# Attention and the first two experts' weights moved into the list schedule, first blocks in smaller steps, token group 0 always visited first

## The chip, the cores and the metric

One core of a Trainium2 chip runs the whole program: TensorE (PE) for matmuls, VectorE (DVE), ScalarE (ACT) and GpSimd (POOL) for elementwise work, SyncE (SP) for issuing most transfers. The metric is the time on the device in microseconds (us), as the median of three runs. Beside it stands one execution taken with the hardware profiler, whose trace the rows below come from.

## The reference

Three layers follow one another on 2 x 576 = 1152 tokens of width 512: attention over a window of 64 keys, four experts that are all used and weighted by gate probabilities, and a layer that multiplies by a cosine of itself.

```python
scores = scale * np.matmul(q, k.transpose(0, 1, 3, 2))
mask = (rel >= 0) & (rel < window)                # window = 64
attn = softmax(np.where(mask, scores, -1e9))
x = np.matmul(attn, v)                            # 2 x 8 heads x 576 x 64, then 1152 x 512
for e in range(4):                                # w1: 512 x 1024, w2: 1024 x 512
    out += p[:, e:e + 1] * (np.maximum(x @ w1[e], 0.0) @ w2[e])
h = out @ w_in                                    # 512 x 2048
y = (h * np.cos(h)) @ w_out                       # 2048 x 512
```

## The kernel before

**Precision.** Each factor of a large matmul is held as a high and a low part, and a product is three matmuls: high by high, high by low, low by high. A weight (name `raw`) is loaded in float32, its high part (`whi`) is a rounding copy, its low part (`wlo`) the difference.

**Attention.** The 1152 tokens are 18 blocks of 64 queries. For a pair of blocks the scores `pss` (L261) are 16 small matmuls from `kT` and `qt`, where `qt` is the query tile `qraw` in another order (function `att_r`). Per block then follow the scaled and masked scores `s` and their maximum `nm` on VectorE (`att_m`), the exponential `e` with its sums on ScalarE (`att_e`), a reciprocal `ri`, the scaling of `e` on GpSimd (`att_n`), four transposes into `pst` (L310), their copy `pt` out of PSUM, and per pair the values `psv` (L325, 16 small matmuls), which become the high and low half of x (`xhi`, `xlo`).

**Experts.** Each of the four experts and the cosine layer are cut into units of 512 hidden columns: units 0 and 1 are the first expert, 2 to 7 the other three, 8 to 11 the cosine layer. Units 0 and 1 run in the plain way: `emit_a` gives twelve matmuls into `ph` (L432 to L434, L629), `emit_b` three per tile of 128 tokens into `pb_acc` (L470), over three token groups of 256, 384 and 512. From unit 2 on the first product is built from seven products of half size (`y` and `seed`, L1038) with sums of weights (`w7hi`, `w7lo`) and of tokens (`tsum`, `thi`, `tlo`), over two token groups, 0 of 640 and 1 of 512 tokens (products with 320 and 256 columns); the second product is `pb_acc` again (L1232). Between unit 7 and unit 8 the sum over the experts is transposed (`psx`, L1304) to become the new x.

**What sets the order.** Each engine runs its instructions in the order in which they are written and waits at the first one that is not ready. The program has two parts. Up to a step in the last token group of the first expert the order is a hand-written list, the string `ORDER`: each token is a load, a step of attention, a weight half, or a point where the next piece of an expert's matmuls goes (`piece`). `W10` in it is ten filler matmuls (`keep_busy`, L241, `idle_ps`, 128 ones by 128 ones). After that point a list scheduler takes over: each group of instructions is a `Job` with an engine, an assumed duration, what it depends on and the buffers that it takes; `plan` lays the jobs out by their latest start times, with TensorE's jobs in the order of `pe_list` and up to eight ahead, `rehearse` replays a plan with small random delays, and the best of 120 plans is emitted. In that second part `visits` sets which token group of a unit comes first, and it alternates:

```python
    for c in range(SPL, NX):
        ks = (0, 1) if (c % 2 == 0) == (c < NM) else (1, 0)
        visits += [(c, k) for k in ks]
```

**Loads.** The SP queue issues most transfers, in the order of the list; ScalarE's queue issues the first chunk of k and two of the q tiles.

Of the kernel before, what the change touches and what calls it, by code (L numbers as in the profile page):

```python
# [27 lines left out]
def tile_window_attention_moe_cosglu(  # L28
# [14 lines left out]
    B, H, D, S = k.shape  # L43
    NTOK = B * S
# [84 lines left out]
    def split_hi(n, copy=nc.scalar.copy):  # L129
        hi = w_tile(n, "hi")  # L130
        copy(out=hi, in_=raw_t[n])
        w_hi[units[n]] = hi

    half_lo = {}


    def split_lo(n, engine, part=None):
        t, hi = raw_t[n], w_hi[units[n]].bitcast(F32)
        if n not in half_lo:
            half_lo[n] = w_tile(n, "lo")  # L140
        lo = half_lo[n]
        c = t.shape[1] // 2
        cs = slice(None) if part is None else slice(c * part, c * (part + 1))
        engine.tensor_tensor(out=lo[:, cs], in0=t[:, cs], in1=hi[:, cs], op=ALU.subtract)
        if part != 0:
            raw_t.pop(n)
            w_lo[units[n]] = half_lo.pop(n)

    actx = ExitStack()
    kp = actx.enter_context(tc.tile_pool(name="kp", bufs=2))  # L150
    vp = actx.enter_context(tc.tile_pool(name="vp", bufs=4))
# [10 lines left out]
    NQ, NVB = 4, 4  # L162
# [3 lines left out]
    def load_q(j):  # L166
        b, i = divmod(j, BPB)
        t = qp.tile([P, W, NP], F32, tag="qraw", name="qraw")
        queue = nc.scalar if 1 < j < 4 else nc.sync
        queue.dma_start(out=t, in_=q[b, i].rearrange("h d n p -> (h d) n p"))  # L170
        q_t[j] = t

    def att_r(j, copy=nc.gpsimd.tensor_copy):
        t = q_t.pop(j)
        qt = qp.tile([P, NP, W], F32, tag="qt", name="qt")
        copy(out=qt.rearrange("d p n -> d n p"), in_=t)
        qt_t[j] = qt


    KCH = [(0, 3), (4, 6), (7, 8), (9, 11), (12, 14), (15, 17)]  # L180
    KMAX = 5 * W


    def load_k(c):
        a, z = KCH[c]
        b, s = divmod(a * W, S)
        s1 = s + (z + 1 - a) * W
        o = 2 * W - nkeys(a)
        t = kp.tile([P, NP, KMAX], F32, tag="kT", name="kT")
        if o:  # L190
            nc.vector.memset(t[:, :, :o], 0.0)
        (nc.sync if c else nc.scalar).dma_start(
            out=t[:, :, o:(z + 2 - a) * W],
            in_=k[b].rearrange("(p h) d s -> (h d) p s", h=2)[:, :, s - W + o:s1],
        )
        for j in range(a, z + 1):
            k_t[j] = t[:, :, (j - a) * W:(j - a + 2) * W]

    def load_v(j):
        n = nkeys(j)  # L200
        b, s = divmod(j * W, S)
        t = vp.tile([P, H * D], F32, tag="vr", name="vr")
        if n < P:
            nc.vector.memset(t[:P - n], 0.0)
        nc.sync.dma_start(out=t[P - n:], in_=v[b, s + W - n:s + W, :])
        v_t[j] = t
# [60 lines left out]
    def att_m(u):  # L267
        pv = ss_t.pop(u)
        b = u - u % 2
        mask = masks[tuple(c for c in range(2) if (b + c) % BPB == 0)]  # L270
        s = sp.tile([P, NP, 2 * W], F32, tag="s", name="s", bufs=3)
        nc.vector.scalar_tensor_tensor(
            out=s, in0=pv, scalar=SCALE, in1=mask.to_broadcast([P, NP, 2 * W]),
            op0=ALU.mult, op1=ALU.min,
        )
        nm = smp.tile([P, NP], F32, tag="nm", name="nm")
        nc.vector.tensor_reduce(out=nm, in_=s, op=ALU.max, axis=AX.X, negate=True)
        s_t[u] = (s, nm)

    def att_e(u):  # L280
        s, nm = s_t.pop(u)
        e = sp.tile([P, NP, 2 * W], F32, tag="e", name="e", bufs=4)
        sm = smp.tile([P, NP], F32, tag="sm", name="sm")
        for p in range(NP):
            nc.scalar.activation(
                out=e[:, p], in_=s[:, p], func=AF.Exp, bias=nm[:, p:p + 1], scale=1.0,
                accum_out=sm[:, p:p + 1],
            )
        r = smp.tile([P, NP], F32, tag="r", name="r")
        nc.scalar.activation(out=r, in_=sm, func=AF.Identity, bias=bias_e, scale=1.0)  # L290
        e_t[u], sm_t[u] = e, r
# [3 lines left out]
    def att_i(u):  # L295
        r = sm_t.pop(u)
        ri = smp.tile([P, NP, 1], F32, tag="ri", name="ri")
# [3 lines left out]
    def att_n(u):  # L301
        e, ri = e_t.pop(u), ri_t.pop(u)
        nc.gpsimd.tensor_tensor(out=e, in0=e, in1=ri.to_broadcast([P, NP, 2 * W]), op=ALU.mult)
        pn_t[u] = e

    def att_t(u):
        pn = pn_t.pop(u)
        ps = bank("pst").rearrange("m (p t) -> m p t", p=NP)
        for p in range(NP):
            nc.tensor.transpose(out=ps[:, p], in_=pn[:, p], identity=ident)  # L310
        ps_t[u] = ps

    def att_p(u, copy=nc.vector.tensor_copy):
        pt = sp.tile([P, NP, P], F32, tag="pt", name="pt", bufs=3)
        copy(out=pt, in_=ps_t.pop(u))
        pt_t[u] = pt

    def att_v(u):
        pts, vts = ([t.pop(u - 1 + c) for c in range(2)] for t in (pt_t, v_t))
        ps = bank("psv") if u * W >= GS[0] else psb.tile([P, 512], F32, tag="psb", name="psv")  # L320
        pv = ps.rearrange("m (p t) -> m p t", p=NP)
        for c in range(2):
            for p in range(NP):
                for h in range(2):
                    nc.tensor.matmul(  # L325
                        out=pv[W * h:W * (h + 1), p, W * c:W * (c + 1)],
                        lhsT=vts[c][:, P * p + W * h:P * p + W * (h + 1)],
                        rhs=pts[h][:, p, W * c:W * (c + 1)],
                        start=True, stop=True,
                    )  # L330
        o_t[u] = pv

    def att_xhi(u):
        pv, at = o_t[u], (u - 1) * W
        k = max(i for i in range(2) if S0[i] <= at)
        if at == S0[k]:
            x_tiles(k)
        hi, lo = (tokens(x[k], k, (at - S0[k]) // P) for x in (xhi, xlo))
        o_t[u] = pv, hi, lo
        nc.scalar.copy(out=hi, in_=pv)  # L340

    def att_xlo(u):
        pv, hi, lo = o_t.pop(u)
        nc.vector.tensor_tensor(out=lo, in0=pv, in1=hi.bitcast(F32), op=ALU.subtract)


# [52 lines left out]
    queues = {"h": [], "j": [], "f": []}  # L399
    script = []  # L400

    def side(kind, fn, *args):
        if script:
            queues[kind].append((fn, args))
        else:
            fn(*args)


    def piece():
        while script:  # L410
            x = script.pop(0)
            if x == ".":
                break
            token(x)
        if not script:
            for kind in queues:
                while queues[kind]:
                    fn, args = queues[kind].pop(0)
                    fn(*args)

    def emit_a(s):
        e, g, f = steps[s]
# [1359 lines left out]
```

## Time and profile before

| | us |
|---|---|
| median of three runs (629.33 to 630.48) | 630.41 |
| profiled execution | 630.69 |
| its span, first to last instruction | 628.9 |
| PE busy | 620.4 (99%) |
| PE weight loads busy | 551.0 (88%) |
| VectorE busy | 477.9 (76%) |
| ScalarE busy | 337.0 (54%) |
| GpSimd busy | 146.9 (23%) |
| chain that ended last, share of PE | 81% |

An engine's busy time is the time in which at least one of its instructions runs by the profile. Matmuls overlap, and their ends are modelled, so a matmul's own duration is longer than its share of PE's time; the spacing from one start to the next is that share. An f32 matmul shows as two records, an instruction with high and low parts (fp32r) as one. The 1.8 us between the span and the execution's own time lie around the program.

### The profile page before, as it was taken

What the parts mean: (1) busy time and instruction counts of PE and PEld (TensorE: products, weight loads), DVE (VectorE), ACT (ScalarE), POOL (GpSimd) and SP (SyncE); (2) the same over time, 40 slices, a digit from 0 to 9 for tenths busy, and PEclk for the clock granted to TensorE, in tenths of its full rate; (3) what the DMA queues carried; (4) which work ended last, traced back from release to release, by engine and by line L of the source; (5) the groups of instructions that cost most, each with busy time, mean ns of one, the idle gap of its engine ahead of it and who ended that gap; (6) DMA issues with size and microseconds to landing.
All of it is one profiled execution on the core that took longest, in us unless ns stands there. A gap on an engine that the chain in (4) does not pass through costs nothing.

```text
span 628.9 us, 10809 instructions
## 1 busy us (share of the span) xinstructions
PE 620.4 (99%) x4019; PEld 551.0 (88%) x4019; DVE 477.9 (76%) x1002; ACT 337.0 (54%) x840; POOL 146.9 (23%) x157
## 2 busy tenths in 40 slices
PE   8999999999999999999999999999899999999997
PEld 7888898888899999889989888988799899999896
DVE  5858639435989999799899999686966578686664
ACT  5958414222354353244343343457988978678653
POOL 6985102310020103210300100323214133112000
PEclk9999999999999999999999999999999999999999
DMA  9943201420145645644534653102202212000022
GB/s 294 299 148 101 86 1 62 126 114 1 27 142 137 204 146 153 174 132 162 166 103 135 203 165 120 50 31 70 68 1 68 68 35 67 2 1 2 0 68 83
DMA packets 37254, 63.10 MB, mean 100 GB/s; under 512 B 2761, under 2 KB 18633, under 8 KB 37202
## 3 DMA queue, kind: packets, MB, share of 16 engines
q1 hardware_dynamic: 36386, 61.63, 31.2%
q10 hardware_dynamic: 816, 0.79, 0.4%
q8 instruction: 31, 0.51, 0.3%
q14 instruction: 21, 0.17, 0.1%
HBM read 51.66 MB, written 10.75 MB: 99 GB/s over the span
## 4 chain that ended last, share of the span: by engine, by line
PE 81%; DVE 11%; DMA 3%; ACT 2%; issue 2%; POOL 1%; ACTq 0%; DVEq 0%; SPq 0%; POOLq 0%
PE pb_acc L1232 33%; PE y L1038 17%; PE seed L1038 13%; PE pb_acc L470 8%; PE ph L629 4%; PE psv L325 1%; PE ph L432 1%; PE ph L433 1%; PE ph L434 1%; DMA raw<-in_moe_w_dram 1%; DVE acc L481 1%; PE pst L310 1%; PE pss L261 1%; DVE x L766 1%; DVE m L744 1%
## 5 line engine op out<-in xcount | busy, mean ns | idle before, releaser
L1232 PE MATMUL pb_acc<-whi,hh 128*128 128x512 f32 x360 | 141.7, 394 | 0.0
L1232 PE MATMUL pb_acc<-wlo,hh 128*128 128x512 f32 x360 | 141.6, 393 | 0.0
L1232 PE MATMUL pb_acc<-whi,hl 128*128 128x512 f32 x360 | 140.4, 390 | 0.0
L1038 PE MATMUL y<-xhi,w7hi 128*128 128x256 f32 (+1 forms) x320 | 95.0, 297 | 1.1 <-DVE hl L1173 1.1
L1038 PE MATMUL y<-xhi,w7lo 128*128 128x256 f32 (+1 forms) x320 | 94.6, 295 | 0.0
L1038 PE MATMUL y<-xlo,w7hi 128*128 128x256 f32 (+1 forms) x320 | 94.4, 295 | 0.0
L1232 PEld LDWEIGHTS pb_acc<-whi,hl 128*128 128x128 f32 x360 | 67.6, 188 | 15.5
L1232 PEld LDWEIGHTS pb_acc<-whi,hh 128*128 128x128 f32 x360 | 67.7, 188 | 9.4
L1232 PEld LDWEIGHTS pb_acc<-wlo,hh 128*128 128x128 f32 x360 | 67.8, 188 | 8.7
L1038 PE MATMUL seed<-thi,w7hi 128*128 128x320 f32 (+1 forms) x240 | 71.7, 299 | 1.0 <-ACT seed L1052 0.9
L1038 PE MATMUL seed<-thi,w7lo 128*128 128x320 f32 (+1 forms) x240 | 70.7, 295 | 0.0
L1038 PE MATMUL seed<-tlo,w7hi 128*128 128x320 f32 (+1 forms) x240 | 70.6, 294 | 0.0
L1038 PEld LDWEIGHTS y<-xhi,w7hi 128*128 128x128 f32 x320 | 60.3, 188 | 3.5 <-DVE hl L1173 1.8
L1038 PEld LDWEIGHTS y<-xlo,w7hi 128*128 128x128 f32 x320 | 60.3, 189 | 1.6
L1038 PEld LDWEIGHTS y<-xhi,w7lo 128*128 128x128 f32 x320 | 60.2, 188 | 0.0
L919 POOL TENSOR_TENSOR wlo<-raw,whi 128x512 fp32r<-128x512 f32 x22 | 29.1, 1333 | 114.4 <-ACT whi L914 48.5
L1038 PEld LDWEIGHTS seed<-thi,w7hi 128*128 128x128 f32 x240 | 45.1, 188 | 7.4 <-ACT seed L1052 1.1
L481 DVE SCALAR_TENSOR_TENSOR acc<-pb_acc,gate_p,acc 128x512 f32<-128x512 f32 x63 | 46.0, 746 | 5.7 <-PE pb_acc L1232 5.6
L1038 PEld LDWEIGHTS seed<-tlo,w7hi 128*128 128x128 f32 x240 | 45.1, 188 | 3.8
L1038 PEld LDWEIGHTS seed<-thi,w7lo 128*128 128x128 f32 x240 | 45.1, 188 | 0.0
L875 POOL TENSOR_TENSOR w7lo<-raw,w7hi 128x256 fp32r<-128x256 f32 (+1 forms) x18 | 16.6, 926 | 117.4 <-DVE sums L851 49.3
L870 ACT CAST w7hi<-sums 128x512 fp32r<-128x512 f32 x40 | 24.8, 622 | 27.4 <-DVE sums L851 24.8
(142 smaller groups left out, 1314.9 us busy)
## 6 DMA issues: line engine op xcount, KB each, us to landing
raw<-in_moe_w_dram SPq DMA_DIRECT2D x32, 512.0 KB, 5.1
raw<-in_moe_w_in_dram SPq DMA_DIRECT2D x16, 512.0 KB, 4.3
w<-x SPq DMA_DIRECT2D x32, 256.0 KB, 4.4
raw<-in_moe_w_out_dram SPq DMA_DIRECT2D x16, 512.0 KB, 4.1
raw<-w SPq DMA_DIRECT2D x16, 512.0 KB, 3.4
vr<-in_v_dram SPq DMA_DIRECT2D x16, 256.0 KB, 3.8
out_dram<-acc SPq DMA_DIRECT2D x18, 128.0 KB, 1.7
qraw<-in_q_dram SPq DMA_DIRECT2D x16, 128.0 KB, 3.8
```

The lines of the kernel that those rows point to most:

```text
L261: nc.tensor.matmul(out=out[h][W * c:W * (c + 1), p], lhsT=qts[c][rows, p, :], rhs=kts[c][rows, p, :], start=True, stop=True,)
L310: nc.tensor.transpose(out=ps[:, p], in_=pn[:, p], identity=ident)
L325: nc.tensor.matmul(out=pv[W * h:W * (h + 1), p, W * c:W * (c + 1)], lhsT=vts[c][:, P * p + W * h:P * p + W * (h + 1)], rhs=pts[h][:, p, W ...
L432: nc.tensor.matmul(out=ps, lhsT=whi[:, d, cs], rhs=xh[:, d, :], start=d == 0, stop=False)
L470: nc.tensor.matmul(out=ps, lhsT=a, rhs=b, start=first and m == 0, stop=last and m == 2)
L481: nc.vector.scalar_tensor_tensor(out=a, in0=ps, scalar=p, in1=a, op0=ALU.mult, op1=ALU.add)
L629: nc.tensor.matmul(out=ps, lhsT=a[:, d, cs], rhs=b[:, d, :], start=d == 0 and m == 0, stop=d == KD - 1 and m == 2,)
L870: nc.scalar.copy(out=operand(w_hi[x], i), in_=part(i))
L875: return engine.tensor_tensor(out=operand(w_lo[x], i), in0=part(i), in1=operand(w_hi[x], i).bitcast(F32), op=ALU.subtract,)
L919: return engine.tensor_tensor(out=w_lo[x][:, i], in0=box["t"][:, i], in1=w_hi[x][:, i].bitcast(F32), op=ALU.subtract,)
L1038: nc.tensor.matmul(out=ps, lhsT=a[:, WI[i], d, :], rhs=b[:, d, :], start=start and d == 0 and m == 0, stop=d == 1 and m == 2, skip_group_c ...
L1232: nc.tensor.matmul(out=ps, lhsT=a, rhs=b[:, fo, :], start=first and fo == 0 and m == 0, stop=last and fo == 1 and m == 2,)
```

## The change

The hand-written order, its tokens and the functions `emit_a`, `emit_b`, `piece` and `side` are gone. All loads, all steps of attention, the gate, the weight halves and the matmuls of units 0 and 1 become jobs, and the list scheduler orders the whole program. In detail:

- A job may now have a choice of engines, each with its own assumed duration (`choice`): the query copy goes to GpSimd, VectorE or ScalarE, the scaling and the low weight halves to GpSimd or VectorE, the copies out of PSUM and the high weight halves to VectorE or ScalarE. `follows` keeps jobs of one kind in order.
- The first chunk of k is cut in two (two blocks each, three buffers in place of two) and moves to the SP queue; q tiles 1 and 3 are issued by ScalarE. The zeroed tiles of both batches are written when the scheduler puts them, which is at the start.
- Block 0's scores are masked and raised to the exponential in two halves of heads; for blocks 2 and 3 the sums of the exponentials are taken on VectorE, and scaling, transposes and copies go in halves; the values of blocks 2 and 3 go in halves.
- An `emit_a` step becomes two jobs of six matmuls, an `emit_b` step one job per tile of 128 tokens.
- Latest start times of the jobs before the first product come from a table of numbers, `DUE`.
- Filler is emitted in front of a TensorE job as long as no expert matmul has been, in a number taken from the gap in the plan.
- Before unit 8 token group 0 is now always first; from unit 8 on the alternation starts with group 0.

```diff
-    KCH = [(0, 3), (4, 6), (7, 8), (9, 11), (12, 14), (15, 17)]
-    KMAX = 5 * W
+    KCH = [(0, 1), (2, 3), (4, 6), (7, 8), (9, 11), (12, 14), (15, 17)]
+    KMAX = 4 * W
...
+    def choice(on, fn, deps=(), new=(), use=()):
+
+        eng = next(iter(on))
+        j = job(eng, on[eng][0], fn, deps, new, use)
+        j.on = on
+        return j
...
+    SPLIT_M, PLAIN, SPLIT_T, SPLIT_V = {0}, {2, 3}, {2, 3}, {2}
...
+    for j in range(NBK):
+        raw, qt = Hold(qraws), Hold(qts)
+        a = in_row("q", load(360.0 if j in (1, 3) else 450.0, lambda j=j: load_q(j), new=[raw]))
+        q_ready[j] = in_row("R", choice(
+            {"POOL": (640.0, True), "DVE": (600.0, True), "ACT": (620.0, False)},
+            lambda engine, j=j: att_r(j, engine), [a], new=[qt], use=[raw],
+        ))
+        q_hold[j] = qt
...
+    for j in range(NBK):
+        hold, pad = Hold(vrs), None
+        if nkeys(j) == W:
+            pad = job("DVE", 480.0, lambda j=j: v_pad(j), new=[hold])
+        v_ready[j] = load(
+            350.0 * nkeys(j) / W, lambda j=j: load_v(j), [pad], new=() if pad else [hold],
+            use=[hold] if pad else (),
+        )
+        in_row("v", v_ready[j])
+        v_hold[j] = hold
...
+            ts = halves(b in SPLIT_T)
+            for h in ts:
+                th = Hold(banks)
+                n = in_row("N", choice(
+                    {"POOL": (1060.0, True), "DVE": (594.0, True)} if h is None else
+                    {"POOL": (560.0, True), "DVE": (330.0, True)},
+                    lambda engine, b=b, h=h: att_n(b, engine, h), [r], use=[eh],
+                ))
+                t = in_row("T", pe(
+                    420.0 / len(ts), lambda b=b, h=h: att_t(b, h), [n],
+                    new=[th] if h else [th, pt_hold[i]], use=[eh], tail=270.0,
+                ))
+                att_list.append(t)
...
-        a = pe(12 * mm_ns(n), matmuls, new=[hold])
-        h = job("ACT", act_ns(n), high, [a, std_b.get(s - 4)], use=[hold])
+        a = pe(6 * mm_ns(n), matmuls(0), [*(x[0] for x in xs), ws[0]], new=[hold])
+        b = pe(6 * mm_ns(n), matmuls(1), [a, *(x[-1] for x in xs), ws[1]], use=[hold])
+        h = job("ACT", act_ns(n), high, [b, *std_b.get(s - 4, ())], use=[hold])
...
+    attended = job(None, 0.0, swap_att, [*jobs_att()])
...
-        ks = (0, 1) if (c % 2 == 0) == (c < NM) else (1, 0)
+        ks = (0, 1) if c < NM or c % 2 == 0 else (1, 0)
...
-    x_ready[SPL, 0] = t_jobs(0, lambda a, w: [])
+    x_ready[SPL, 0] = t_jobs(0, lambda a, w: [attended, *std_as])
...
+    FIRST = {"ACT": 2800.0, "DVE": 500.0, "POOL": 4300.0}
...
+    DUE = """
+        -45602 -30292 -29876 -41701 -27795 6858 -13322 -9131 13255 692 -17507 15025 -10703
...
     for j in sorted(jobs, key=lambda j: (began[j], rank[j])):
-        made = j.fn(nc.vector if j.eng == "DVE" else nc.gpsimd) if j.size else j.fn()
+        if j.eng == "PE":
+            if began[j] < began[pe_list[0]]:
+                keep_busy(int((began[j] - stopped) * 0.8 / 110.0))
+            stopped = began[j] + j.ns
+        made = j.fn(engine_of[j.eng]) if j.on else j.fn()
```

On TensorE the program began with these rows, up to the first values (`psv`):

```order
L241 MATMUL idle_ps<-idle 128x128 x10
L261 MATMUL pss<-kT,qt 64x128 x16
L241 MATMUL idle_ps<-idle 128x128 x5
L261 MATMUL pss<-kT,qt 64x128 x16
L241 MATMUL idle_ps<-idle 128x128 x6
L261 MATMUL pss<-kT,qt 64x128 x16
L310 MATMUL pst<-ident,e 128x128 x4
L360 MATMUL psg<-ident,dpn 128x9 x4
L241 MATMUL idle_ps<-idle 128x128 x2
L310 MATMUL pst<-ident,e 128x128 x4
L241 MATMUL idle_ps<-idle 128x128 x3
L325 MATMUL psv<-pt,vr 64x64 x16
```

Now TensorE begins with these, to the same point and the block of filler behind it:

```order
L233 MATMUL idle_ps<-idle 128x128 x31
L253 MATMUL pss<-kT,qt 64x128 x16
L233 MATMUL idle_ps<-idle 128x128 x12
L253 MATMUL pss<-kT,qt 64x128 x16
L233 MATMUL idle_ps<-idle 128x128 x21
L315 MATMUL pst<-ident,e 128x128 x4
L233 MATMUL idle_ps<-idle 128x128 x7
L315 MATMUL pst<-ident,e 128x128 x4
L233 MATMUL idle_ps<-idle 128x128 x8
L328 MATMUL psv<-pt,vr 64x64 x16
L315 MATMUL pst<-ident,e 128x128 x4
L233 MATMUL idle_ps<-idle 128x128 x7
```

The third scores (`pss`) and the gate (`psg`) have moved behind the first values, and the blocks of filler are fewer and longer: 86 instructions in these six, where there were 33 in eight (the last three, of 4, 1 and 2, stood behind the first values).

On the SP queue the first transfers were these (q, expert weights, v, k, gate):

```order
L170 DMA qraw<-in_q_dram 128x256 x2
L117 DMA raw<-in_moe_w_dram 128x4x256
L205 DMA vr<-in_v_dram 64x512
L205 DMA vr<-in_v_dram 128x512
L170 DMA qraw<-in_q_dram 128x256 x2
L192 DMA kT<-in_k_dram 128x4x256
L205 DMA vr<-in_v_dram 128x512
L352 DMA dpn<-in_moe_domain_probs_dram 9x512
```

and now they are these:

```order
L150 DMA qraw<-in_q_dram 128x256 x2
L181 DMA kT<-in_k_dram 128x4x128
L196 DMA vr<-in_v_dram 64x512
L196 DMA vr<-in_v_dram 128x512
L181 DMA kT<-in_k_dram 128x4x192
L118 DMA raw<-in_moe_w_dram 128x4x256
L196 DMA vr<-in_v_dram 128x512
L118 DMA raw<-in_moe_w_dram 128x2x512
```

The first chunk of k, half as large, has come over from ScalarE's queue to the third place, and the first weight has moved behind the second chunk.

At the handover to the cosine layer, on TensorE, the second pair of products of the first cosine unit ended before like this (`psx`: transposes of the new x):

```order
L1038 MATMUL y_5048<-xlo,w7hi 128x256
L1038 MATMUL y_5048<-xhi,w7lo 128x256
L1304 MATMUL psx<-ident,acc 128x128 x4
L1038 MATMUL seed_5058<-thi,w7hi 128x256
L1038 MATMUL seed_5058<-tlo,w7hi 128x256
```

and ends now like this:

```order
L1130 MATMUL y_5141<-xhi,w7lo 128x320
L1396 MATMUL psx<-ident,acc 128x128 x4
L1324 MATMUL pb_acc<-whi,hh 128x512
L1324 MATMUL pb_acc<-wlo,hh 128x512
L1324 MATMUL pb_acc<-whi,hl 128x512
L1324 MATMUL pb_acc<-whi,hh 128x512
L1324 MATMUL pb_acc<-wlo,hh 128x512
L1324 MATMUL pb_acc<-whi,hl 128x512
L1130 MATMUL seed<-thi,w7hi 128x320
```

Six expert matmuls now stand between the transposes and the seed's product, and the products there are those of token group 0, with 320 columns.

## Rows read from the trace of the kernel before

**Rows 1.** Stages: wall us, busy us (instructions) of PE, PEld, DVE, ACT, POOL, clock.
```profile
0.00:25.07 25.07, 23.08 (x318) 20.01 (x318) 15.92 (x39) 18.01 (x63) 19.38 (x40) 1.00 0.94 301
...
70.00:135.00 65.00, 65.00 (x333) 55.18 (x332) 36.77 (x71) 20.91 (x51) 14.27 (x14) 1.00 0.17 56
135.00:425.00 290.00, 289.87 (x1696) 260.53 (x1696) 253.61 (x509) 118.70 (x263) 43.42 (x36) 1.00 0.41 126
425.00:450.00 25.00, 22.99 (x146) 19.86 (x145) 20.39 (x58) 21.09 (x57) 6.78 (x8) 1.00 0.27 83
...
625.20:628.90 3.70, 0.00 (x0) 0.00 (x0) 0.75 (x2) 0.00 (x0) 0.00 (x0) 1.00 0.42 140
```

**Rows 2.** Groups by line and form on PE: records, busy us, mean ns, idle before.
```profile
L1232 PE MATMUL pb_acc<-whi,hh 128*128 128x512 f32 x360 | 141.7, 394 | 0.0
...
L1038 PE MATMUL y<-xhi,w7hi 128*128 128x320 f32 x160 | 49.6, 310 | 1.1 <-DVE hl L1173 1.1
...
L470 PE MATMUL pb_acc<-whi,hh 128*128 128x512 f32 x72 | 29.0, 403 | 0.0
...
L241 PE MATMUL idle_ps<-idle 128*128 128x128 f32 x66 | 11.2, 326 | 1.1 <-DVE idle L237 1.1
```

**Rows 3.** Chain in order of time, three pieces: start us, us, what.
```profile
151.84 1.76 PE y L1038 x12
...
156.74 1.39 PE pb_acc L1232 x6
...
292.42 1.42 PE y L1038 x12
```

**Rows 4.** PE's timeline to the first expert matmul: start, us, instruction, idle before.
```profile
1.08 4.63 PE L241 MATMUL idle_ps<-idle 128*128 128x128 f32 x20 [1.08 <-DVE idle L237]
5.65 1.58 PE L261 MATMUL pss<-kT,qt 64*64 64x128 f32 x32
7.16 1.38 PE L241 MATMUL idle_ps<-idle 128*128 128x128 f32 x10
...
11.75 1.10 PE L261 MATMUL pss<-kT,qt 64*64 64x128 f32 x32
13.05 0.66 PE L310 MATMUL pst<-ident,e 128*128 128x128 f32 x4 [0.20 <-POOL e L303]
...
17.55 0.66 PE L310 MATMUL pst<-ident,e 128*128 128x128 f32 x4
18.04 1.06 PE L241 MATMUL idle_ps<-idle 128*128 128x128 f32 x8
...
21.29 1.15 PE L325 MATMUL psv<-pt,vr 128*64 128x64 f32 x32
22.37 0.66 PE L310 MATMUL pst<-ident,e 128*128 128x128 f32 x4
22.96 1.10 PE L261 MATMUL pss<-kT,qt 64*64 64x128 f32 x32
23.99 1.15 PE L325 MATMUL psv<-pt,vr 128*64 128x64 f32 x32
25.07 0.39 PE L432 MATMUL ph<-xhi,whi 128*128 128x256 f32 x1
```

**Rows 5.** PE's timeline at the handover to the cosine layer: two matmuls that waited.
```profile
440.86 0.38 PE L1038 MATMUL seed<-thi,w7hi 128*128 128x256 f32 x1 [0.88 <-ACT seed L1052]
449.21 0.41 PE L1038 MATMUL y<-xhi,w7hi 128*128 128x320 f32 x1 [1.09 <-DVE hl L1173]
```

**Rows 6.** Weight loads of the filler: a block of six; durations of all, min/median/max.
```profile
10.21 1.42 PEld L241 LDWEIGHTS idle_ps<-idle 128*128 128x128 f32 x12 [0.17 <-issue]
...
L241 PEld LDWEIGHTS idle_ps<-idle x66: 186/192/333, 1.1 to 21.0; 128*128 128x128 f32 x66
```

**Rows 7.** ScalarE's timeline: the last input of the first scores.
```profile
5.45 0.63 ACT L176 COPY qt<-qraw 128x256 f32<-128x256 f32 x1 [1.90 <-DMA qraw<-in_q_dram]
```

**Rows 8.** The page's transfers: issues, KB each, median us to landing, for v.
```profile
vr<-in_v_dram SPq DMA_DIRECT2D x16, 256.0 KB, 3.8
```

More of the change, by code (lines that the diff above doesn't have):

```diff
@@ L299, in att_i @@
         ri_t[u] = ri
[L301 to L316, printed above, removed]
@@ L529, in tile_window_attention_moe_cosglu @@
     make_mask(())
-    for x in ORDER.split():
-        script.extend(x if x[0] == "." else [x])
-    T2 = 2 * SPL * 2 * NFC - 5
-    for what, s in seq[:T2 + 1]:
-        (emit_a if what == "A" else emit_b)(s)
-    assert not script and not any(queues.values())
-    actx.close()
+    make_mask((1,))
     class Job:
-        __slots__ = ("eng", "ns", "fn", "deps", "new", "at", "late", "n", "out", "tail", "port", "size")
+        __slots__ = ("eng", "ns", "fn", "deps", "new", "at", "late", "n", "out", "tail", "port", "on", "spare", "follows")
     jobs = []
@@ new lines, in load, with halves, in_row @@
+    def load(ns, fn, deps=(), new=(), use=()):
+        j = job("SP", ns, fn, deps, new, use, tail=2000.0)
+        j.spare = 300.0
+        return j
+    NBK = NB
+    SPLIT_M, PLAIN, SPLIT_T, SPLIT_V = {0}, {2, 3}, {2, 3}, {2}
+    row_of = {}
+    def halves(two):
+        return (0, 1) if two else (None,)
+    def in_row(name, j):
+        j.follows = row_of.get(name, ())
+        row_of[name] = (j,)
+        return j
+    qraws, qts, kts, vrs = Slots(NQ), Slots(NQ), Slots(NK), Slots(NVB)
+    ss, es, pts = Slots(3), Slots(4), Slots(3)
@@ L903, in w2_jobs @@
             war = [
[L904 to L905 removed]
+                b for s, (e, g, f) in enumerate(steps)
+                if (e, f // 2) == old and g == NG - 1 for b in std_b[s]
             ]
@@ L1494, in gap, with plan @@
         if a.eng == "SP":
-            return a.tail + SPARE
+            return a.tail + a.spare
         return AGAIN[a.eng] if a.eng == b.eng else a.tail
-    def plan(starts, jitter):
+    DUE = """
[34 rows of a table added]
+    """
+    first_jobs = (j for j in jobs if j.n < first_seed.n and j.eng is not None)
+    fixed = {j: 10.0 * int(t) for j, t in zip(first_jobs, DUE.split(), strict=True)}
+    for j in jobs:
+        for h in j.new:
+            h.of = sum(x.slots is h.slots for x in j.new)
+    def plan(starts, jitter, limit=1e9):
         line = list(pe_list)
@@ L1563, in plan @@
                 arrive(j)
-        busy = dict.fromkeys(engines, 0.0)
+        busy = dict.fromkeys(engines, 0.0) | FIRST
         began, events, now, done = {}, [(0.0, -1, None)], 0.0, 0
         seen, port, owner = 0, 0.0, "POOL"
+        for t in FIRST.values():
+            seen += 1
+            heapq.heappush(events, (t, seen, None))
         todo = list(pe_list)
```

612 lines of the change are left out of this document (334 added, 278 removed), and 33 rows, old and new, of the table DUE.

## The prediction, made before the change was run

> **What bounds the kernel now.** I read the page first, then busy time by stage, then TensorE's (PE's) timeline of the first 26 us, then its waits. By stage [rows 1], PE is busy for 289.87 of 290 us between 135 and 425 us, with VectorE at 253.61 and the others far below: the long middle is a queue of matmuls that nothing interrupts, and no edit to the other engines' order can shorten it. What is not matmul work lies in four places: the first 25.07 us, in which PE also runs filler; 25.07 to 70 us, where attention is woven into the first experts; 425 to 450 us, where the last gated expert hands over to the cosine layer (22.99 busy of 25); and 3.7 us after the last matmul. Busy time flatters the first of these, because filler counts as busy: one line, L241, multiplies ones by ones [rows 2]. So I count PE's time by spacing, start to start, and not by the busy column.
>
> The work itself, from counts [rows 2] and spacings [rows 3]: 3 x (360 + 72) = 1296 expert matmuls with 512 columns at 1.39/6 = 0.232 us give 300.3; 840 products with 320 columns (3 x 160 y and 3 x 120 seed) at 1.76/12 = 0.147 and 840 with 256 at 1.42/12 = 0.118 give 222.6; 96 ph of each of three widths (by the order of instructions) at 0.118, 0.174 (my interpolation) and 0.232 give 50.4. Attention has 9 score groups of 1.03 us (22.96 to 23.99), 18 transpose groups of 0.49 (17.55 to 18.04) and 9 value groups of 1.08 (21.29 to 22.37) [rows 4]; with 9 later transposes and the gate that is 33. Sum 606. The span of 628.9 is then 1.1 of start, 606 of work, 10.7 of filler, 3.7 of tail and about 7 of waits. Stage by stage the same count puts the waits at 2.3 before 25.07 us (25.07 less 1.1 of start, 10.7 of filler and 10.9 of four score, six transpose and three value groups and the gate), about 2.2 up to 70 us and 2.8 between 425 and 450 us, where two rows name the largest [rows 5].
>
> **What the change does to PE.** The order of the changed kernel holds the same 606 us of matmuls, since every group occurs equally often; so work cancels, and two terms are left: filler and waits.
>
> Filler, the largest term. Before, there are 33 filler matmuls in eight blocks; after, 86 in six, 31, 12, 21, 7, 8 and 7, all ahead of the first expert matmul. They are counted by the new line keep_busy(int(gap * 0.8 / 110.0)): 110 ns for one. The trace has another price. Each of the 33 shows as two records (66) [rows 2], because an f32 matmul passes twice. In a block of six the loads of the twelve passes start 0.112 us apart, (1.42 - 0.19)/11 [rows 6], so one filler matmul takes 0.224 us and a block some 0.2 more at its edge (10.21 + 12 x 0.112 = 11.55, and the next matmul starts at 11.75 [rows 4]). In the first block the passes are slower still: 20 of them from 1.08 to 5.65 us, 0.229 each, twice the later spacing, although the granted clock reads 1.00 throughout [rows 1, 4]. I take that as the 1.2 GHz level, which PE leaves after about 4.6 us of uninterrupted filler; the new first block starts in the same way.
>
> The Trainium skill, "TensorE: Matmul & The Clock Gate", section "Back-to-back issue gap", gives about 81 ns for each pair of weight load and matmul with 128 columns. The rows here say 112; at 81 the forecast below would be some 4.7 us lower, an estimate from that page, still slower than now. The measurement decides.
>
> So PE's walk through the new order is: 31 filler, ten slow (to 5.65) and 21 x 0.224 + 0.2 = 4.9, put the first scores at 10.5 us instead of 5.65; scores 1.03; 12 filler 2.9; scores; 21 filler 4.9; the first transposes at 20.4 instead of 13.05; then 0.5 + 1.8 + 0.5 + 2.0, values at 25.2, 1.1 + 0.5 + 1.8, a transpose in halves around scores and gate 2.0, values 1.1, scores 1.0: 32.7. First expert matmul about 33.2, against 25.07 [rows 4], and with two transpose groups and one value group (2.1 us) less behind it. Filler sums to 22.9 us against 10.7: +12.1.
>
> Does the filler lie beside waits that would be there anyway? Only in part. The last input of the first scores, a q copy on ScalarE, starts at 5.45 us and ends at 6.08 [rows 7]; the new queues load q0 to q3 and only half as many bytes of k ahead of it, so the scores could start by 6.1 and stand 4.4 us behind ones times ones. From the end of the first scores (7.16) to the first transposes (13.05) the chain of mask, maximum, exponential, reciprocal and scaling took 5.9 us [rows 4, 7]; from 11.6 it would be done by 17.5, and PE comes at 20.4. What the change does on that chain is therefore beside the filler and worth nothing at this place: half steps for block 0, sums taken on VectorE for blocks 2 and 3, q copies by VectorE and ScalarE and no longer GpSimd, the third mask made early. If the filler were short, they would save perhaps 1 us.
>
> Waits. The 2.3 us before 25.07 vanish behind the filler. Two new ones are possible there: the two padded tiles for batch 1 are taken at the start, so the fourth value load now waits for the first value group (26.3 us) and lands some 3.8 us later [rows 8], about 30.1, and the values that need it come at 30.6; and the first expert matmul waits for the last output copies. I take 0.5 (0 to 2). The 2.2 between 25 and 70 us I halve to 1.1 (0 to 6): all that does not hang on PE (loads, weight halves, q copies) runs 8 us ahead of it by then, and the finer pieces (a half of four K steps, one token tile) give the order more to fill with; against it the attention stretches over more of the first experts. Handover, 2.8: the alternating visits had the next unit's first matmuls follow a bare pair of products, and seed waited 0.88 and y 1.09 [rows 5]. With token group 0 always first, six expert matmuls (1.39) stand ahead of that seed and products are 320 wide (0.88 for six, not 0.71). I take 1.4 (0 to 4). The tail is unchanged: more tiles in the last unit, but each store is cut as before, 3.7.
>
> Sum: +12.1 filler, -1.8, -1.1, -1.4 of waits = +7.8. On the profiled span 628.9 that is 636.7, with the 1.8 us around it (630.69 - 628.9) 638.5, and the runs' median lies 0.3 below the profiled execution: **638.2 us**.
>
> **Rivals.** (1) No waits are left after the first expert matmul: -2.2 and -2.8 in place of -1.1 and -1.4, 635.7 us. For it: the middle of the trace shows that a good order leaves none. Against: 2.8 of them stand at a change of layers, where chains are long. (2) The late attention makes the first gated expert of the product form late. Its tiles may be built only when attention has given back its memory; from the last value group to the first product there are 54.6 us now (79.9 to 134.5) and by the same count of work 38 after. If half of the lost 16 us shows, +8: 646.2. Against it: VectorE is busy only 36.77 of 65 us between 70 and 135 [rows 1]. (3) Not slower: the filler is as short as the kernel's formula has it, 0.11 us each, because its two passes overlap better in long blocks. Then 4.6 + 76 x 0.11 + 1.2 = 14.2, +3.5, less 4.3 of waits: 629.6 us, no change or a little faster. It decides below some 0.12 us for one warm filler matmul; twelve passes at 0.112 each speak against it.
>
> Even with all waits gone, +12.1 - 7 is above zero: that, and not the size of the gain elsewhere, fixes the sign.
>
> **Numbers.** Forecast 0.64, rival 1 0.18, rival 2 0.13, rival 3 0.05. The range runs from 634.5 (rival 1 and a block less of filler) to 645.0 (about half of rival 2); outside lie rival 3 and the rest of rival 2, 0.12. About 0.2% (1.3 us) is what a measurement can tell from no change: faster 0.04, same 0.03, both from rival 3 and a remainder for what I have not seen; slower 0.93.
>
> **What would show it.** In the changed profile: 172 filler records and about 23 us from their blocks; the first scores near 10.5, the first transposes near 20.4, values near 25.2, the first ph near 33 us; no idle of PE ahead of the scores and transposes (it comes from filler straight into them), and VectorE, ScalarE and GpSimd idle there instead; between 440 and 465 us less than 2 us of waits; the middle as full as now. I am wrong if the first ph stands before 28 us, or if the filler's passes are nearer than 0.09 us; and the forecast is right for a wrong reason if the first ph is near 25 and the loss lies behind 70 us.

## The result: 1.4% slower, and the profile after

The changed kernel takes 639.53 us (median of four runs, 639.33 to 639.64) and the kernel before 630.44 us on the same chip (four runs, 629.33 to 631.78): a ratio of 1.0143, 95% interval 1.0123 to 1.0163. The forecast was 638.2 us, with a range of 634.5 to 645.0. Its profiled execution took 639.33 us, with a span of 637.5 us (628.9 before).

Five landmarks on PE say where the 8.6 us of span came from. Each is the start of the first or last instruction of its kind:

| PE reaches, us | before | after | lost on the way |
|---|---|---|---|
| first scores (`pss`) | 5.65 | 10.72 | +5.07 |
| first transposes (`pst`) | 13.05 | 20.45 | +2.33 |
| first expert matmul (`ph`) | 25.07 | 32.31 | -0.16 |
| first product (a `seed` of one matmul) | 134.31 | 142.84 | +1.29 |
| last matmul | 624.81 | 633.53 | +0.19 |

The last two are these rows of PE's timeline, first of the kernel before, then of the changed one (after the last matmul there are 4.1 us left before and 4.0 after):

```profile
134.31 0.39 PE L696 MATMUL seed<-xhi 128*128 128x512 f32 x1
...
624.81 0.39 PE L1232 MATMUL pb_acc<-whi,hl 128*128 128x512 f32 x1
```

```profile
142.84 0.39 PE L784 MATMUL seed<-xhi 128*128 128x512 f32 x1
...
633.53 0.39 PE L1324 MATMUL pb_acc<-whi,hl 128*128 128x512 f32 x1
```

Two transpose groups and one value group (2 x 0.49 + 1.08 = 2.1 us [rows 4]) have moved from the third stretch into the fourth. On equal work PE has lost 9.3 us by its first expert matmul, gets 0.8 back up to the first product, and runs level from there.

PE's timeline of the changed kernel answers to [rows 4]:

```profile
1.08 9.71 PE L233 MATMUL idle_ps<-idle 128*128 128x128 f32 x62 [1.08 <-DVE idle L229]
10.72 1.10 PE L253 MATMUL pss<-kT,qt 64*64 64x128 f32 x32
11.75 2.94 PE L233 MATMUL idle_ps<-idle 128*128 128x128 f32 x24
14.63 1.10 PE L253 MATMUL pss<-kT,qt 64*64 64x128 f32 x32
15.66 4.96 PE L233 MATMUL idle_ps<-idle 128*128 128x128 f32 x42
20.45 0.60 PE L315 MATMUL pst<-ident,e 128*128 128x128 f32 x4
20.89 1.73 PE L233 MATMUL idle_ps<-idle 128*128 128x128 f32 x14
22.45 0.60 PE L315 MATMUL pst<-ident,e 128*128 128x128 f32 x4
22.89 1.95 PE L233 MATMUL idle_ps<-idle 128*128 128x128 f32 x16
24.77 1.15 PE L328 MATMUL psv<-pt,vr 128*64 128x64 f32 x32
25.85 0.66 PE L315 MATMUL pst<-ident,e 128*128 128x128 f32 x4
26.35 1.73 PE L233 MATMUL idle_ps<-idle 128*128 128x128 f32 x14
27.91 0.38 PE L315 MATMUL pst<-ident,e 128*128 128x128 f32 x2
...
32.31 0.39 PE L686 MATMUL ph<-xhi,whi 128*128 128x256 f32 x1
```

Six blocks stand there, and after the first instruction no row has a wait in brackets: PE goes from filler straight into scores and transposes. From start to start the blocks take 9.64, 2.88, 4.79, 1.56, 1.88 and 1.56, together 22.3 us, against 10.7 before. The group of these rows answers to the last one of [rows 2]:

```profile
L233 PE MATMUL idle_ps<-idle 128*128 128x128 f32 x172 | 23.0, 297 | 1.1 <-DVE idle L229 1.1
```

The other engines stand meanwhile. The changed kernel's stage from 6 to 12 us (columns as in [rows 1]) has 0.06 us of VectorE and nothing on ScalarE and GpSimd:

```profile
6.00:12.00 6.00, 6.00 (x75) 5.71 (x75) 0.06 (x1) 0.00 (x0) 0.00 (x0) 1.00 1.06 355
```

The scores' last input, the first chunk of k, is there by 5.95 to 6.64 us (e5, e1 and e2 below wait for it), 4 us before the scores. VectorE's timeline shows its first mask, which waited 7.46 us for them, and the mask of the third block, which waited 0.91 us for the second scores behind their own 12 filler matmuls:

```profile
11.94 0.42 DVE L271 SCALAR_TENSOR_TENSOR s<-pss,mask 128x256 f32<-128x256 f32 x1 [7.46 <-PE pss L253]
...
15.84 0.69 DVE L271 SCALAR_TENSOR_TENSOR s<-pss,mask 128x512 f32<-128x512 f32 x1 [0.91 <-PE pss L253]
```

GpSimd's timeline shows the two scalings, of block 0 and block 1. They end at 18.53 and 20.08, 1.9 and 2.4 us before PE leaves its filler for the transposes that need them:

```profile
17.49 1.04 POOL L308 TENSOR_TENSOR e<-e,ri 128x512 f32<-128x512 f32 x1 [12.35 <-DVE ri L303]
19.04 1.04 POOL L308 TENSOR_TENSOR e<-e,ri 128x512 f32<-128x512 f32 x1 [0.51 <-DMA kT<-in_k_dram]
```

By stage (columns as in [rows 1]) the middle is as full as it was, and the handover as empty: 48.10 busy of 50 us, against 47.99 in the kernel before, whose row stands second:

```profile
135.00:425.00 290.00, 289.60 (x1679) 259.36 (x1677) 251.21 (x506) 115.58 (x259) 31.72 (x27) 1.00 0.43 133
425.00:475.00 50.00, 48.10 (x286) 42.34 (x285) 42.46 (x111) 38.32 (x88) 1.30 (x1) 1.00 0.10 32
```

```profile
425.00:475.00 50.00, 47.99 (x286) 42.54 (x285) 38.01 (x99) 42.81 (x107) 12.46 (x15) 1.00 0.14 42
```

PE's timeline of the changed kernel around the handover answers to [rows 5]; the seed's wait has grown from 0.88 to 1.05, and in place of y's 1.09 there are two smaller ones. Apart from the 1.08 us at the start, PE has one more named wait in the whole run, 0.40 us at 333 us:

```profile
434.04 0.47 PE L1324 MATMUL pb_acc<-whi,hh 128*128 128x512 f32 x1 [0.46 <-DVE xlo L1421]
450.68 0.65 PE L1396 MATMUL psx<-ident,acc 128*128 128x128 f32 x4 [0.25 <-DVE acc L415]
453.78 0.41 PE L1130 MATMUL seed<-thi,w7hi 128*128 128x320 f32 x1 [1.05 <-ACT seed L1144]
```

### The profile page after: what moved, and what is told of

Read it like the earlier page. It is cut to its first block, busy times and chain, and to the rows that moved or that the text cites. A ratio compares the mean times of both kernels' runs of the same rounds, so it can differ in the third digit from the quotient of the medians.

```text
span 637.5 us, 11011 instructions
## 1 busy us (share of the span) xinstructions
PE 630.4 (99%) x4125; PEld 561.6 (88%) x4125; DVE 479.2 (75%) x1020; ACT 344.4 (54%) x849; POOL 122.1 (19%) x133
## 4 chain that ended last, share of the span: by engine, by line
PE 42%; DVE 7%; ACT 2%; issue 0%; DVEq 0%; ACTq 0%
PE pb_acc L1324 23%; PE y L1130 11%; PE seed L1130 8%; DVE hl L1223 1%; DVE w7lo L967 1%; DVE acc L415 1%; DVE tsum L1471 1%; DVE sums L943 1%; ACT xhi L1411 0%; DVE x L850 0%; DVE xlo L1421 0%; DVE x L861 0%; DVE x L856 0%; ACT kk L1251 0%; DVE tsum L1480 0%
## 5 line engine op out<-in xcount | busy, mean ns | idle before, releaser
L1130 PE MATMUL y<-xhi,w7hi 128*128 128x320 f32 (+1 forms) x320 | 94.9, 296 | 0.0
L1130 PE MATMUL y<-xhi,w7lo 128*128 128x320 f32 (+1 forms) x320 | 94.6, 296 | 0.0
L1130 PE MATMUL y<-xlo,w7hi 128*128 128x320 f32 (+1 forms) x320 | 94.5, 295 | 0.0
L1011 POOL TENSOR_TENSOR wlo<-raw,whi 128x512 fp32r<-128x512 f32 x18 | 23.3, 1297 | 153.9 <-DVE wlo L1011 43.6
L841 ACT ACTIVATE raw<-raw 128x512 f32<-128x512 f32 x32 | 21.9, 683 | 36.4 <-DVE m L834 20.6
L1251 ACT ACTIVATE kk<-kk,bias_h 128x320 f32<-128x320 f32 (+1 forms) x64 | 34.4, 537 | 2.1
```

The costliest lines, as they stand in the source:

```text
L841: nc.scalar.activation(out=wh, in_=wh, func=AF.Abs)
L1011: return engine.tensor_tensor(out=w_lo[x][:, i], in0=box["t"][:, i], in1=w_hi[x][:, i].bitcast(F32), op=ALU.subtract,)
L1130: nc.tensor.matmul(out=ps, lhsT=a[:, WI[i], d, :], rhs=b[:, d, :], start=start and d == 0 and m == 0, stop=d == 1 and m == 2, skip_group_c ...
L1251: nc.scalar.activation(out=own["r"], in_=own["r"], func=AF.Sin, bias=bias_h, scale=-TWO_PI)
```

## The experiments

Theory A: filler is priced at half its length and stands in front of ready work. Theory B: the new order is slow by itself, and filler only fills waits. Every run stands against the kernel before on its own chip (medians of 630.0 to 630.3 us). The rows come from four chips, so a small difference between two rows is best read from their ratios. The columns from `pss` to "end" are from one profiled execution each; "end" is the time from the first product to the last matmul:

| run | first `pss` | first `pst` | first `ph` | first product | end | median | ratio (95%) |
|---|---|---|---|---|---|---|---|
| e1_priced | 6.64 | 13.48 | 24.31 | 136.12 | 490.69 | 632.96 | 1.0050 (1.0038 to 1.0062) |
| e2_first_block | 6.58 | 16.32 | 28.18 | 139.88 | 490.68 | 636.70 | 1.0107 (1.0093 to 1.0121) |
| e3_visits | 9.88 | 19.61 | 31.47 | 143.37 | 489.32 | 638.42 | 1.0128 (1.0115 to 1.0141) |
| e4_w31 | 10.27 | 16.80 | 29.06 | 138.14 | 490.45 | 633.32 | 1.0050 (1.0037 to 1.0063) |
| e5_ten | 5.95 | 13.38 | 25.45 | 137.24 | 490.70 | 634.12 | 1.0064 (1.0052 to 1.0077) |
| e6_best | 6.61 | 13.46 | 24.29 | 138.45 | 489.35 | 631.52 | 1.0021 (1.0012 to 1.0029) |
| e7_unsplit | 7.05 | 13.66 | 26.15 | 138.21 | 490.77 | 634.86 | 1.0073 (1.0055 to 1.0091) |
| e8_k_early | 6.69 | 13.54 | 24.35 | 135.82 | 490.75 | 633.28 | 1.0044 (1.0031 to 1.0057) |
| e9_no_filler | 6.54 | 14.57 | 27.02 | 138.02 | 490.73 | 634.65 | 1.0064 (1.0052 to 1.0076) |
| e10_best2 | 7.29 | 14.14 | 24.97 | 136.63 | 489.32 | 631.58 | 1.0024 (1.0013 to 1.0035) |
| e11_before_rule | 5.65 | 13.03 | 25.29 | 134.19 | 489.62 | 629.51 | 0.9989 (0.9980 to 0.9998) |
| e12_reseed | 5.65 | 12.59 | 24.84 | 134.38 | 490.65 | 630.30 | 1.0005 (0.9996 to 1.0014) |

**Filler at its own price (e1).**

```diff
-                keep_busy(int((began[j] - stopped) * 0.8 / 110.0))
+                keep_busy(int((began[j] - stopped) * 0.8 / 224.0))
```

> The changed kernel with one number altered: filler is counted with 224 ns for one matmul, in place of 110, so its six blocks have 15, 6, 10, 3, 4 and 3 (41, not 86). Theory A (filler stands in front of work that is ready): first scores at 6.8 us (was 11.75 minus scores, 10.72), then the chain of mask, exponential and scaling (6.8 us from the first scores' end) sets the first transposes at 14.6 (was 20.45), with a wait of about 1.7; of the later blocks 2.3 us go and 1 comes back as waits; first expert matmul about 25, time 632 us (630 to 634). Theory B (the new order itself is slow, filler only fills waits): the same gaps stand open as waits, first expert matmul near 32, 639.5 us.

632.96 us: theory A. The order of everything else is the same, and 6.6 of the 9.1 us are gone. In its timeline PE now comes to its inputs a little early, with a short wait behind a block where there was none:

```profile
1.08 4.97 PE L233 MATMUL idle_ps<-idle 128*128 128x128 f32 x30 [1.08 <-DVE idle L229]
6.64 1.10 PE L253 MATMUL pss<-kT,qt 64*64 64x128 f32 x32 [0.59 <-DMA kT<-in_k_dram]
7.67 1.60 PE L233 MATMUL idle_ps<-idle 128*128 128x128 f32 x12
...
13.48 0.66 PE L315 MATMUL pst<-ident,e 128*128 128x128 f32 x4 [0.74 <-POOL e L308]
...
24.31 0.39 PE L686 MATMUL ph<-xhi,whi 128*128 128x256 f32 x1
...
34.31 1.10 PE L253 MATMUL pss<-kT,qt 64*64 64x128 f32 x30 [1.40 <-DMA kT<-in_k_dram]
```

The first expert matmul comes 8.0 us earlier, the first product only 6.7: the last row, a wait for the chunk of k with blocks 9 to 11, gives 1.3 back. (It is the fifth of seven chunks now; the expectations call it the fourth, which it was in the kernel before.) What is late next is a load.

**The first block alone (e2), and the same block in the kernel before (e4).**

```diff
-                keep_busy(int((began[j] - stopped) * 0.8 / 110.0))
+                keep_busy(int((began[j] - stopped) * 0.8 / 110.0) if stopped else 10)
```

> The changed kernel with its first block of filler cut from 31 to ten and the other five as they are (12, 21, 7, 8, 7). If each block costs its own length as far as it stands behind ready inputs: first scores at 6.6 us when their chunk of k lands, 4.1 us earlier than 10.72, first transposes at 16.4 (no wait, since their chain is done by 13.5), first expert matmul at 28.2; 635.4 us, up to 636.3 where a wait on the fourth chunk of k comes back. If filler were free: 639.5 us.

```diff
-        q0 q1 k0 q2 q3 u0 v0 R0 v1 r1 q4 q5 k1 W10 S0 v2 R2 g R3 u1 M0 C0 u2 q6 q7 M1 W5 S2 E0 v3 u3
+        q0 q1 k0 q2 q3 u0 v0 R0 v1 r1 q4 q5 k1 W31 S0 v2 R2 g R3 u1 M0 C0 u2 q6 q7 M1 W5 S2 E0 v3 u3
```

> The kernel before with its first block of filler at 31 matmuls in place of ten. Theory A: 21 more at 0.224 us, all in front of scores whose last input is there at 6.1 us; the chain behind the first scores moves by as much: first scores at 10.4, first expert matmul at 29.6, time 635.0 us (634.5 to 635.3). Theory B (filler lies in waits that would be there anyway): 630.4 to 631.5 us.

e2: first transposes at 16.32 and first expert matmul at 28.18, both as worked out; 636.70, a little above the 636.3 that I gave as the upper end; 1.21 us come back as a wait at the k chunk. e4, by its timeline below: the block grows from 4.57 to 9.19 us, 21 more in 4.62 us, 0.22 each, and costs the otherwise unaltered kernel 3.2 us; the profiled execution shows 3.8, with the first expert matmul 4.0 later. I expected 4.6, and 633.32 us lies below my range. In the profiled execution the first scores behind the longer block took 1.03 us, not 1.51, and a 0.28 us wait for a query copy behind them has gone.

```profile
1.08 9.26 PE L241 MATMUL idle_ps<-idle 128*128 128x128 f32 x62 [1.08 <-DVE idle L237]
10.27 1.10 PE L261 MATMUL pss<-kT,qt 64*64 64x128 f32 x32
```

**Less and less filler (e5, e9).**

```diff
-                keep_busy(int((began[j] - stopped) * 0.8 / 110.0))
+                keep_busy(0 if stopped else 10)
```

and, for e9, in place of the same line:

```diff
+                keep_busy(0)
```

> The changed kernel with a first block of ten filler matmuls and no other filler. Theory A: first scores at 5.65 us as in the kernel before, first transposes at 13.5 after a wait, first expert matmul at 22 to 24, time 630 us (628 to 632); if the waits bring TensorE's clock down, the later spacing of matmuls doubles for some us and the time is 632 to 636. Theory B: 639.5 us, with waits where the filler was.

> The changed kernel without any filler. If filler only delays: as the run with filler counted at 224 ns or better, 631 to 633 us, with waits in its place. If filler also holds TensorE's clock up: the granted clock reads 0.5 through most of the first 21 us as in the run with ten filler matmuls, matmuls there take twice as long, and the time is 634 to 637 us.

Both are slower than e1, which has 41 filler matmuls: by 1.2 and 1.7 us in the medians (0.9 for both by the ratios, whose intervals overlap with e1's). The landmarks show it more clearly: the first transposes of e5 come 0.1 us earlier than those of e1, its first expert matmul 1.1 us later. The stages of e5 show why: the granted clock reads 0.50 (1.2 GHz) from 12 to 20 us, after PE had stood 1.14 and 3.50 us in front of its second scores and its first transposes (the timeline behind the stages), and these transposes take 1.12 us where e1's take 0.66.

```profile
12.00:14.00 2.00, 0.62 (x3) 0.63 (x4) 1.59 (x6) 2.00 (x9) 1.04 (x1) 0.50 1.10 348
...
18.00:20.00 2.00, 2.00 (x32) 1.88 (x31) 1.26 (x3) 0.52 (x2) 0.60 (x2) 0.50 0.36 98
```

Its timeline:

```profile
8.77 1.10 PE L253 MATMUL pss<-kT,qt 64*64 64x128 f32 x32 [1.14 <-DMA kT<-in_k_dram]
13.38 1.12 PE L315 MATMUL pst<-ident,e 128*128 128x128 f32 x4 [3.50 <-POOL e L308]
...
17.79 1.97 PE L328 MATMUL psv<-pt,vr 128*64 128x64 f32 x30 [1.11 <-DVE pt L154]
```

So filler inside a wait pays, by about 1 us here, and filler beyond it is a delay. For e9 I was right on the time and wrong on the view: the passes take twice as long up to 23 us, but the granted clock reads 1.00 there (last section).

**The chain edits (e7).** On e1's order, blocks 2 and 3 sum on ScalarE and block 0 goes in one piece:

```diff
-                    "DVE", 1315.0 if h is None else 785.0, lambda b=b, h=h: att_m(b, h), [s],
+                    "DVE", 1315.0 if h is None else 785.0, lambda b=b, h=h: None if h else att_m(b), [s],
...
-                    lambda b=b, h=h, plain=plain: att_e(b, h, not plain), [m],
+                    lambda b=b, h=h: None if h else att_e(b), [m],
...
-                a = job("DVE", 594.0, lambda b=b: att_z(b), [e], use=[eh])
+                a = job("DVE", 594.0, lambda: None, [e], use=[eh])
```

> The run with filler counted at 224 ns, with its order kept and two of the change's edits on the attention chain undone in place: block 0 is masked and exponentiated in one piece, not in halves of heads, and the sums of the exponentials of blocks 2 and 3 come from ScalarE again. The forecast's step (with short filler the edits save perhaps 1 us): first transposes near 14.2 us (13.48 with the edits), 634.0 us. Rival (the chain from the end of the first scores to the first transposes took 5.9 us in the kernel before and 5.8 with the edits, so they save nothing): 13.5 us and 633.0 us.

Neither as told. The first transposes are no later (13.66 at a start that was 0.4 later), so for them the edits are worth nothing. The second transposes are later, and in the timeline of e7 PE is slower behind their wait (1.08 us for the transposes, where e1's take 0.66):

```profile
16.35 1.08 PE L315 MATMUL pst<-ident,e 128*128 128x128 f32 x4 [1.37 <-POOL e L308]
17.22 1.92 PE L233 MATMUL idle_ps<-idle 128*128 128x128 f32 x8
```

In e1 that wait is 0.45 us. With short filler the edits are worth some 0.9 us at this place. By the medians they are worth 1.9 and by the ratios 1.4, with intervals that overlap (e7's runs spread over 4 us); in the profiled execution the rest is 0.4 us of a later start, which differs between executions, and matmuls at a lower clock (0.57 from 16 to 20 us).

**The k chunk (e8).** On e1's order, the load of the chunk with blocks 9 to 11 is put 6 us earlier in the plan, past one weight, three v and three q loads:

```diff
+    began[k_ready[9]] -= 6000.0
```

> The run with filler counted at 224 ns, with one load moved: the fourth chunk of k is issued some 4 us earlier on the SP queue. If TensorE's wait of 1.40 us at 34.31 us is due to the late issue alone: no wait there and 631.6 us. Rival (the q, v and weight loads that it overtakes come late instead, or the transfers share their rate): 632.5 to 633.5 us.

633.28 us, no gain. PE no longer waits for k, and 2 us later its timeline has a wait for the low half of a weight:

```profile
36.57 0.39 PE L686 MATMUL ph<-xhi,wlo 128*128 128x256 f32 x1 [1.13 <-POOL wlo L651]
```

This is not the rival's price for overtaking, since the weight is no later than it was. VectorE's timeline has the copy into its high half, which waits for the load to land, at 33.10 us in e1 (first row) and at 33.16 in e8 (second):

```profile
33.10 0.69 DVE L154 CAST whi<-raw 128x1024 fp32r<-128x1024 f32 x1 [1.65 <-DMA raw<-in_moe_w_dram]
```

```profile
33.16 0.70 DVE L154 CAST whi<-raw 128x1024 fp32r<-128x1024 f32 x1 [1.57 <-DMA raw<-in_moe_w_dram]
```

GpSimd begins the low half at 33.92 and 33.99. In e1 PE stood at the k chunk while this went on; in e8 it comes earlier and meets the weight as the next limit.

**The rule for token groups (e3, e11, e12).** In the changed kernel the old rule, in the kernel before the new one (the first edit below, the other way round), and in the kernel before only another seed:

```diff
-        ks = (0, 1) if c < NM or c % 2 == 0 else (1, 0)
+        ks = (0, 1) if (c % 2 == 0) == (c < NM) else (1, 0)
```

```diff
-            draw = random.Random(n)
+            draw = random.Random(n + 1000)
```

> The changed kernel with the old rule for which token group comes first (alternating before unit 8); the filler stays 31, 12, 21, 7, 8 and 7. Theory A, as the forecast had it: the handover to the cosine layer costs 1.4 us more again, 640.9 us. Rival: the handover lost as much in the changed kernel (3.0 us, by work counted against the trace between 425 and 475 us) as before, so the rule is worth nothing, 639.5 us (639 to 640).

> The kernel before with the new rule alone (token group 0 always first before unit 8, then alternating from group 0), all else as it was. The forecast's step on the handover: 1.4 us faster, 629.0 us, with less than 1.5 us of waits between 425 and 475 us. By the runs on the changed kernel (489.3 us from the first product to the last matmul with the old rule, 490.7 with the new one): 1.4 us slower, 631.7 us. If the rule only changes which plan the scheduler finds: 630.3 us or any other time within 1.5 us of it.

> The kernel before with nothing altered but the seed of the random offsets from which the list scheduler makes its 120 plans (the old rule stays). If the rule for token groups moves the stretch from the first product to the last matmul by itself (489.6 us with the new rule, 490.5 with the old one): 490.5 us there and 630.2 us. If any new search of plans moves it by about 1 us, whatever the rule: another length between 489.3 and 491, and other waits between 425 and 475 us than the 0.88 and 1.09 us of the kernel before.

In the kernel before the new rule (e11) is better, by 0.9 us in the end (489.62 for 490.50) and by 0.1% in the whole. In the changed kernel it is worse, by 1.4 us (490.69 for 489.32); e3 shows only part of that in its time, since it also waits for the k chunk, as e1 and e2 do (1.4 us more than the changed kernel up to the first product), and had a first block of filler 0.8 us shorter; 638.42 us fits neither of its expectations. A new seed with the old rule leaves the length (490.65 us, time 630.30), as if the rule set it, though with other waits. That is one seed in one kernel: in the changed kernel each rule was run with one plan only, so whether the 1.4 us there belong to the rule or to the two plans found is not shown. Work counted against the trace, as in the forecast, puts what is lost between the first product and the end at about 2.4 us before, 2.6 after, 1.3 in e3 and 1.6 in e11, most of it around 425 to 460 us; the differences are firmer than the levels. PE's timeline has these waits there, first in e3, then in e11:

```profile
449.32 0.39 PE L1130 MATMUL seed<-thi,w7hi 128*128 128x256 f32 x1 [0.59 <-ACT seed L1144]
457.97 0.42 PE L1130 MATMUL y<-xhi,w7hi 128*128 128x320 f32 x1 [0.46 <-DVE hl L1265]
```

```profile
425.57 0.47 PE L1232 MATMUL pb_acc<-whi,hh 128*128 128x512 f32 x1 [0.24 <-DVE xlo L1329]
443.26 0.42 PE L1038 MATMUL seed<-thi,w7hi 128*128 128x320 f32 x1 [1.74 <-ACT seed L1052]
```

The two waits of e11 come to 1.98 us, as much as the two of [rows 5], and more than the 1.5 us that the forecast's step allowed. So its 0.9 us are not in the waits that the rows name, and the run does not confirm the step as it was told, although the time went its way.

**The best of it (e6, e10).** e6 is e1 with the old rule and the earlier k chunk; e10 moves the chunk by 3 us only and leaves out the last block of filler:

```diff
+    began[k_ready[9]] -= 3000.0
+    blocks = iter((15, 6, 10, 3, 4, 0))
...
-                keep_busy(int((began[j] - stopped) * 0.8 / 224.0))
+                keep_busy(next(blocks) if began[j] - stopped > 300.0 else 0)
```

> The run with filler counted at 224 ns, the fourth chunk of k issued earlier and the old rule of alternating token groups. From the shares seen so far (1.4 us for the rule by the time from the first product to the last matmul, 489.3 against 490.7 us, and 1.4 us for the k chunk): 630.2 us (629.5 to 631.0), no measurable difference from the kernel before. Rival (by the forecast, token group 0 first is better by 1.4): 633 us.

> The run with filler at 224 ns, the earlier k chunk and the old rule, with two numbers altered: the k chunk is moved by half as much (past one q, one v and one weight load only), so that the weight it had overtaken comes less late (TensorE waited 1.13 us for its low half, or for the k chunk 1.40 before the move), and the last block of filler (three) is left out. About 0.5 us each: 630.5 us (630.0 to 631.4), the same as the kernel before within what can be told. If the transfers of that stretch are limited by their rate, any order of them leaves a wait of 1 us: 631.0 to 631.5 us.

631.52 and 631.58 us, both above my ranges: the old rule gives its 1.4 us again, the load nothing. PE waits 2.12 us for the low half of the weight in e6 and 1.40 in e10. (The profiled execution of e6 took 633.61 us, 2.1 above its median, so its first product at 138.45 us may be later than in its other runs.) The two kernels are 8 us better than the changed one and still 0.2% above the kernel before. The only version below that is the small one, e11, by 0.1% (0.9980 to 0.9998), less than the 0.2% that the prediction takes as measurable.

## Why the prediction was right, step by step

- **Filler, +12.1: right, +11.6.** The price of 0.224 us for one held (e4: 0.22). The ten slow matmuls at the start held only roughly, since that part differs from run to run (last section): the same block of 31 took 9.64 us here, 8.80 in e3 and 9.19 in e4, so it is partly luck that the first scores came within 0.2 us of the forecast. With 86 times the formula's 0.11 there would have been 9.5 us of it. Rival 3 is out. e1 shows the cause, not only the sum: at the right price the same order is 6.6 us faster.
- **The places**: first scores 10.72 (forecast 10.5), transposes 20.45 (20.4), values 24.77 (25.2), first expert matmul 32.31 (33.2). The 2.1 us of groups, which the forecast calls "less behind it", are less in front of that matmul and more behind; the sum does not use them.
- **The chain beside the filler**: GpSimd's scaling ended at 18.53 us, not at 17.5. VectorE runs in order and stood at the third mask until the second scores came (the 0.91 us above), ahead of block 0's reciprocal. So the filler also lengthened the chain that it covered, from 5.9 us to 6.8; PE came later still, and the time does not show it.
- **Waits before the first expert matmul, -1.8: mis-sized, -2.3.** I left 0.5 for the v load behind the first values and for the output copies; PE waits for neither.
- **Waits up to the first product, -1.1: -0.8**, as 1.29 is less than the 2.1 us of moved work. Rival 2, the late first product, is out: the seed at 142.84 us has no wait, and in e1 it comes forward with the rest. Rival 1 is out as well, since PE loses as much at the handover as before.
- **Handover, -1.4: wrong, +0.2** from the first product to the end (by busy time the handover itself is level, 48.10 against 47.99 of 50 us). It was worked out from six expert matmuls that stand ahead of one seed now. They do, and that seed still waited 1.05 us. e11 has 0.9 us less with the new rule in the kernel before, e3 1.4 less with the old one in the changed kernel. The rule fixes the order of PE, but the chains on VectorE and ScalarE that the matmuls wait for are planned anew around it; that this is the reason is not shown, and what in the plan makes the difference stays open.
- **Chain edits, nothing beside the filler, 1 us if it were short**: 0.9 us at the second transposes (e7), none at the first.
- **Sum**: the four terms missed by -0.5 and -0.5 (filler, first waits), +0.3 and +1.6, together +0.9; the span is 0.8 above the 636.7 of the sum. That the misses partly cancel is luck: without the first two the sum would have been 1.9 too low.

## What to carry to other kernels

Filler is paid for at what it takes on the chip: read its price from start-to-start spacings before a formula counts it, and keep each block shorter than the wait that it covers. Do not leave it out altogether: with the waits left open the clock fell (e5) or rose late (e9), which took back about 1 us. When a search sets the order, a rule's gain read from one neighbourhood of the trace is not the rule's worth: the kernel with the same rule was 0.9 us better in one case and 1.4 worse in the other, with one plan each. And where a load limits the start, look for the limit behind it before moving that load: here the low half of a weight stood behind the k chunk, and the weight landed at the same time whether k came early or late.

## What the runs showed that I had not expected

Without any filler (e9) PE's first matmuls run at about half their later rate up to 23.9 us, while the granted clock reads 1.00; once it has been up and falls again (e5), the column says 0.50. In these traces only durations and spacings tell the level before the first rise, as e9's timeline (16 score matmuls, two records each, in 1.91 and in 1.10 us) and its stages show:

```profile
22.13 1.91 PE L253 MATMUL pss<-kT,qt 64*64 64x128 f32 x32
...
25.99 1.10 PE L253 MATMUL pss<-kT,qt 64*64 64x128 f32 x32
```

The stages:

```profile
13.00:17.00 4.00, 2.00 (x8) 1.43 (x8) 3.62 (x8) 4.00 (x13) 3.01 (x3) 1.00 1.10 348
...
21.00:24.00 3.00, 3.00 (x39) 2.50 (x37) 1.32 (x3) 2.87 (x6) 1.35 (x2) 1.00 0.72 176
```

And the slow part of the same first block of 31 lasts differently in different runs. The stage from 5 to 6 us, for the filler alone (us, PE busy, PEld busy, clock, DMA), has 7 records in the changed kernel and 12, the full rate, in e3:

```profile
5.00:6.00 1.00, 1.00 (x7) 1.00 (x6) 1.00 0.96 288
```

```profile
5.00:6.00 1.00, 1.00 (x12) 1.00 (x11) 1.00 0.99 278
```

How much of the scatter of the unprofiled runs comes from this is not shown.
